# Reordering an attention and expert-layer kernel: one weight part loaded earlier, batch 0's second layer by parts over four token blocks, batch 2's scores two slots later and batch 3's attention three

## The chip, the cores and the metric

The kernel runs on one core of one Trainium2 chip. The metric is the device time of one execution in microseconds (us); lower is better. Each kernel was run several times and the medians are quoted. A ratio is the mean time of one kernel's fast runs over the mean of the other's fast runs of the same rounds, so it is not quite the ratio of the medians that stand beside it.

A core has a matrix engine (TensorE, "PE" in the profile, its weight loads "PEld"), VectorE ("DVE"), ScalarE ("ACT"), GpSimd ("POOL") and SyncE ("SP"). Each has its own list of instructions in the kernel; semaphores tie the lists together. In the trace TensorE holds to its list's order: in the changed kernel no matmul starts between 53.81 and 56.79 us, while the next of the list waits for `a`.

## The reference

For each of 8 batches and 8 heads there is a cross attention in both directions between 512 tokens `x` and 32 states. The results are stacked into 4352 rows of 512 numbers (8 batches of 512 tokens and 32 states) and go through a layer with 2048 hidden units:

```python
def _attn_ref(x, state):                      # x (8,8,512,64), state (8,8,32,64)
    scores = scale * x @ state^T;  a  = softmax(scores);  xread = a  @ state
    scores2 = scale * state @ x^T; a2 = softmax(scores2); sread = a2 @ x
    return concatenate([xread, sread], axis=2)

def _moe_ref(x, w_in, w_out, s, b):           # x (4352,512), w_in (512,2048), w_out (2048,512)
    h = x @ w_in
    r = maximum(h, 0)
    return (s * (r * r) + b) @ w_out
```

(The matrix products are abridged here; the softmax subtracts the row's maximum.) Outputs and inputs are float32; the kernel works in float16 with float32 sums.

## The kernel before

The program of one batch, in the names that the profile shows:

- `xT`: tokens transposed; by TensorE for batches 0 and 1 (`xTps`), by a transposing DMA later.
- `T` (scores), `E = exp(T)` on ScalarE, `D` (row sums by a matmul with a block of ones), `L = Ln(D)`, `R = exp(-L)`, `a = E*R` on VectorE. This is one chain of five steps over three engines.
- `M` = states times w_in, in four column groups. So the first layer of the tokens is `h = M^T a`, sixteen pieces of two 512-column matmuls: `mm1_x(b, f)`. ScalarE makes `r = relu(h)`, VectorE `g = r*r`.
- Second layer: for batch 0 in sixteen "units" of four 512-column matmuls, one token block and one quarter of w_out each. From batch 1 on by seven half-size products (`oA`, `oB`, `oC`, 112 matmuls of 256 columns), which need sums of quarters of `g` (`s`) and of w_out (`wd`) from VectorE.
- `V`, `sr`, `srT`: the states' own attention; all batches' states go through the layer at the end (names with `_sr`).
- The matmuls of `M` and `T` carry 64*32 in the profile and those of `V` 128*32, where the layers' carry 128*128; the prediction calls the first two kinds quarter-array and the layers' full-array.

TensorE's list is set by hand. "Slot f of batch s" below is the place in its list after `mm1_x(s, f)`. Into the sixteen slots of a batch go the second layer of the batch before and the attention of the batch after:

```python
def pieces(s):                                   # what goes into the slots of batch s, beside the second layer
    nb = s + 1
    if s == 1:
        ...
        at(2, lambda: att_M(1, 2, "act"))
        at(3, bias_sum)
        at(4, bias_end)
        at(3, lambda: att_M(1, 3, "act"))
        at(6, lambda: att_stT(2))
        ...
        at(8, lambda: att_M(2, 0, "act"))
        at(8, lambda: att_M(2, 1, "act"))
        at(10, lambda: att_M(2, 2, "act"))
        at(10, lambda: att_T(2, [0, 1]))
        at(11, lambda: att_ET(2))
        at(12, lambda: att_D(2, [0, 1]))
        at(13, lambda: att_M(2, 3, "act"))
        at(13, lambda: att_V(0))
        return out
    ...
# batch 0's second layer: token block, quarter
    units.append((0, 2 * (i // 8) + i % 2, i % 8 // 2))     # two blocks at a time, all four quarters
# slots of batch 1: one unit in each but 5, 14 and 15; then sixteen matmuls of batch 1's own second layer
    for f in [*range(5), *range(6, 14)]:
        items[f] = [lambda u=todo.pop(0): unit(u)]
    items[14], items[15] = first[0:8], first[8:16]
# loads, one queue, in this order (the first three w_in parts stand ahead of them)
    load_x(1); load_wi(3); load_wo(0..3); states; load_x(2)
```

PSUM, where matmuls write, is used as three pools of two buffers of 128x1024 float32 or less: `psA` for attention, `psH` for `h`, `psO` for the second layer. A buffer is free again when VectorE or ScalarE has copied it out (in e1, below, `h` waits 1.1 us for that).

The softmax here doesn't subtract the row's maximum and nothing guards it: scores larger than these inputs give would overflow.

## Time and profile before

| | value | where it is read |
|---|---|---|
| time | 212.24 us before the prediction (3 runs), 212.37 us in the pair with the change (4 runs) | device times |
| TensorE busy | 202.6 of 209.8 us | page, part 1 |
| TensorE's share of the chain that ended last | 88% | page, part 4 |
| TensorE's waits over 0.15 us | 3.2 us, all before 22 us | table of waits |
| one 512-column matmul at full clock | 0.216 us start to start | timeline |

The page of the kernel before: busy time, share of the span and count of instructions by engine (part 1), and the shares of the chain that ended last by engine (part 4).

```profile
PE 202.6 (97%) x1972; PEld 131.5 (63%) x1972; DVE 155.9 (74%) x286; ACT 132.1 (63%) x226; POOL 37.6 (18%) x64
...
PE 88%; DVE 4%; DMA 3%; ACT 3%; POOL 0%; issue 0%; SPq 0%
```

The table of waits of the kernel before, the three longest of TensorE's six rows: who waited, for whom, us in total, times, longest.

```profile
PE warm_ps L68 <- DVE warm L617: 1.2, 1, 1.2
PE h L68 <- DVE M L263: 0.6, 1, 0.6
PE T L68 <- ACT xT L187: 0.4, 1, 0.4
...
```

All six waits fall into the first 22 us, where w_in still arrives. After that, and until the tail, TensorE never stands idle, which makes the case simple to reason about: waiting time can only be won in the first 22 us (and in the tail), and anything that makes TensorE wait later can be expected to add to the total.

The next view cuts the same execution into stages, from the first matmul of one batch's first layer to the next one's: 0, 1, 2, then 3 to 6 together, then the rest. The columns are the stretch, its length, and for each engine busy us and count, then the granted TensorE clock as a share of full speed, the DMA share and GB/s.

```profile
11.55:27.17 15.62, 14.01 (x119) 5.68 (x118) 11.95 (x22) 13.42 (x26) 3.00 (x4) 1.00 1.28 205
27.17:52.25 25.08, 25.01 (x220) 11.18 (x218) 17.76 (x32) 18.16 (x29) 4.47 (x7) 1.00 1.17 161
52.25:74.81 22.56, 22.56 (x266) 15.27 (x264) 19.03 (x37) 15.89 (x26) 3.49 (x5) 1.00 0.72 125
74.81:162.30 87.49, 87.49 (x918) 59.92 (x916) 68.31 (x121) 63.62 (x105) 12.58 (x18) 1.00 0.50 96
162.30:209.80 47.50, 43.71 (x395) 35.30 (x392) 34.21 (x66) 15.30 (x33) 5.39 (x8) 1.00 0.19 62
```

Stage by stage TensorE's busy time equals the length to within 0.1 us, except in batch 0's stage and in the tail. The 87.49 us are four stages of 21.87 us: the steady state.

Last, the timeline of the kernel before at the chain from D to `a` of batch 2 (start, length, instruction; the rest of that stretch is cut):

```profile
46.26 0.59 PE L68 MATMUL D<-E,bones 128*128 128x512 f16 x2
...
46.95 1.02 ACT L240 ACTIVATE L<-D 128x1024 f32<-128x1024 f32 x1
...
48.00 1.06 ACT L241 ACTIVATE R<-L 128x1024 f16<-128x1024 f32 x1
...
49.09 0.69 DVE L242 TENSOR_TENSOR a<-E,R 128x1024 f16<-128x1024 f16 x1 [0.59 <-ACT R L241]
```

From the start of `D` at 46.26 to the end of `a` at 49.78 are 3.5 us. TensorE has three more slots, 6 us, to work through before batch 2's first layer needs `a` at 52.25, so nobody waits.

### The profile page before, as it was taken

What the parts mean: (1) busy time and instruction counts of PE and PEld (TensorE: products, weight loads), DVE (VectorE), ACT (ScalarE), POOL (GpSimd) and SP (SyncE); (2) the same over time, 40 slices, a digit from 0 to 9 for tenths busy, and PEclk for the clock granted to TensorE, in tenths of its full rate; (3) what the DMA queues carried; (4) which work ended last, traced back from release to release, by engine and by line L of the source; (5) the groups of instructions that cost most, each with busy time, mean ns of one, the idle gap of its engine ahead of it and who ended that gap; (6) DMA issues with size and microseconds to landing.
All of it is one profiled execution on the core that took longest, in us unless ns stands there. A gap on an engine that the chain in (4) does not pass through costs nothing.

```text
span 209.8 us, 4787 instructions
## 1 busy us (share of the span) xinstructions
PE 202.6 (97%) x1972; PEld 131.5 (63%) x1972; DVE 155.9 (74%) x286; ACT 132.1 (63%) x226; POOL 37.6 (18%) x64
## 2 busy tenths in 40 slices
PE   7988999999999999999999999999999999999992
PEld 2434343445666776677666766676667777788882
DVE  0587826978779895779677976698669977895862
ACT  2678865798597549964896479656984454533100
POOL 5870001501011312021111201120111111100210
PEclk9999999999999999999999999999999999999999
DMA  5999996999788393971199209211411111110143
GB/s 177 226 202 206 206 191 106 169 192 161 195 78 125 105 148 66 170 152 67 36 138 181 85 22 181 71 50 53 100 53 50 53 50 50 53 50 0 53 139 113
DMA packets 39289, 23.73 MB, mean 113 GB/s; under 512 B 24228, under 2 KB 37284, under 8 KB 39268
## 3 DMA queue, kind: packets, MB, share of 16 engines
q0 software_dynamic: 15536, 16.19, 40.1%
q1 hardware_dynamic: 22932, 6.88, 19.9%
q10 hardware_dynamic: 800, 0.36, 0.7%
q8 instruction: 15, 0.25, 0.5%
q14 instruction: 6, 0.05, 0.1%
HBM read 17.33 MB, written 8.91 MB: 125 GB/s over the span
## 4 chain that ended last, share of the span: by engine, by line
PE 88%; DVE 4%; DMA 3%; ACT 3%; POOL 0%; issue 0%; SPq 0%
PE h L68 25%; PE oB L68 18%; PE oC L68 12%; PE oA L68 11%; PE o L68 6%; PE Mps L68 4%; PE h_sr L68 3%; DMA xf<-in_x_dram 3%; ACT r L324 2%; PE D L68 1%; PE T L68 1%; PE V L68 1%; PE oB_sr L68 1%; DVE g L330 1%; DVE M L263 1%; PE oA_sr L68 1%
## 5 line engine op out<-in xcount | busy, mean ns | idle before, releaser
L324 ACT ACTIVATE r<-h 128x512 f16<-128x512 f32 x126 | 73.8, 600 | 47.3 <-PE h L68 45.6
L68 PE MATMUL h<-a,M 128*128 128x512 f16 x256 | 75.0, 379 | 0.9 <-DVE M L263 0.6
L330 DVE TENSOR_TENSOR g<-r 128x1024 f16<-128x1024 f16 x64 | 43.9, 688 | 16.0 <-ACT r L324 15.9
L68 PEld LDWEIGHTS <-s 128*128 128x128 f16 x448 | 42.8, 98 | 17.6 <-issue 3.7
L68 PEld LDWEIGHTS <-g 128*128 128x128 f16 x400 | 37.9, 98 | 18.2 <-issue 2.9
L495 POOL DMA_DIRECT2D out_dram<-osb x27 | 18.2, 675 | 127.2 <-DVE osb L487 119.8
L68 PE MATMUL oB<-wd,s 128*128 128x256 f16 x224 | 32.7, 273 | 0.0
L68 PE MATMUL oA<-wo,g 128*128 128x256 f16 x224 | 31.6, 273 | 0.1
L68 PEld LDWEIGHTS <-M 128*128 128x128 f16 x256 | 24.6, 98 | 10.8 <-DVE M L263 1.6
L266 ACT CAST M<-Mps 128x1024 f16<-128x1024 f32 x27 | 26.8, 1019 | 1.4 <-PE Mps L68 0.8
L68 PE MATMUL oC<-wd,s 128*128 128x256 f16 x112 | 16.5, 273 | 0.0
L68 PE MATMUL o<-wo,g 128*128 128x512 f16 x64 | 16.3, 380 | 0.0
L68 PE MATMUL oB<-wd,g 128*128 128x256 f16 x112 | 15.9, 273 | 0.0
L68 PE MATMUL oC<-wo,s 128*128 128x256 f16 x112 | 15.3, 273 | 0.0
L68 PE MATMUL Mps<-wi,stT 64*32 64x512 f16 x256 | 12.2, 383 | 0.0
L324 ACT ACTIVATE r_sr<-h_sr 128x256 f16<-128x256 f32 x16 | 6.1, 382 | 8.4 <-PE h_sr L68 8.4
L68 PEld LDWEIGHTS <-stT 64*32 64x32 f16 x384 | 4.6, 89 | 10.4 <-issue 8.1
L487 DVE SCALAR_TENSOR_TENSOR osb<-oC,s_bc,u 128x512 f32<-128x512 f32 x12 | 9.0, 749 | 2.7 <-PE oC L68 2.7
L430 DVE TENSOR_TENSOR s<-s,g 128x1024 f16<-128x1024 f16 x14 | 9.6, 687 | 0.2
L217 ACT ACTIVATE E<-T 128x512 f16<-128x512 f32 x16 | 9.4, 596 | 0.5 <-PE T L68 0.5
L432 DVE TENSOR_TENSOR s<-g,s 128x1024 f16<-128x1024 f16 x14 | 9.6, 686 | 0.0
L68 PE MATMUL h_sr<-srdT,wi 128*128 128x256 f16 x64 | 9.6, 273 | 0.0
(96 smaller groups left out, 201.1 us busy)
## 6 DMA issues: line engine op xcount, KB each, us to landing
out_dram<-osb POOLq DMA_DIRECT2D x31, 256.0 KB, 2.5
xn<-in_x_dram POOLq DMA_DIRECT2D x7, 512.0 KB, 9.5
wi<-in_moe_w_in_dram POOLq DMA_DIRECT2D x4, 512.0 KB, 9.1
wo<-in_moe_w_out_dram POOLq DMA_DIRECT2D x4, 512.0 KB, 15.9
xf<-in_x_dram SPq DMA_DIRECT2D x2, 512.0 KB, 4.9
out_dram<-osb_sr SPq DMA_DIRECT2D x8, 32.0 KB, 1.6
out_dram<-osb_sr ACTq DMA_DIRECT2D x8, 32.0 KB, 1.7
out_dram<-osb_last SPq DMA_DIRECT2D x2, 128.0 KB
```

The lines of the kernel that those rows point to most:

```text
L68: return nc.tensor.matmul(out, lhsT, rhs, start=start, stop=stop, tile_position=tp, is_transpose=is_transpose, skip_group_check=True,)
L217: nc.scalar.activation(a["E"][:, g, :].rearrange("p (m t) -> p m t", m=2), T[:, :, 256 * i : 256 * i + 256], AF.Exp, scale=scale, accum_ou ...
L263: nc.vector.tensor_copy(dst[:, 0], two[0])
L266: nc.scalar.copy(dst, ps)
L324: nc.scalar.activation(r16[:, f % 2], hps, AF.Relu)
L330: nc.vector.tensor_mul(gt[:, f % 4 - 1 : f % 4 + 1], r16, r16)
L430: nc.vector.tensor_sub(o, SQ[b, 1, j], a11)
L432: nc.vector.tensor_sub(o, a12, SQ[b, 2, j])
L487: nc.vector.scalar_tensor_tensor(osb, acc[bank], s_bc, add, ALU.mult, ALU.add)
L495: nc.gpsimd.dma_start(dst[j][:, :, n0 : n0 + NH], osb)
```

## The change

The intent: with the first w_out quarter loaded early, batch 0's second layer can start while batch 0's first layer still waits for copies, filling TensorE's early idle time. All four token blocks are then worked quarter by quarter, so that each quarter of w_out is used as it lands. Blocks 2 and 3 take one attention PSUM buffer for that long, so attention must make room: batch 2's scores move two slots down in batch 1's slots, part of its other work moves into batch 2's own slots, and there batch 3's attention moves three slots down. The diff, cut to its core:

```diff
@@ loads
         cast_st(nc.gpsimd, 1, 2)
+        load_wo(0)
         load_x(1)
         load_wi(3)
-        for q in range(4):
+        for q in range(1, 4):
             load_wo(q)
+        load_x(2)
         nc.gpsimd.dma_start(out=st16[:, 4:, 0, :], in_=st_v[:, 4:, :])
-        load_x(2)
@@ units: four token blocks, quarter by quarter; blocks 2 and 3 in an attention buffer
-        units.append((0, 2 * (i // 8) + i % 2, i % 8 // 2))
+        units.append((0, i % 4, i // 4))
...
-        if f0 == 0:
+        if f0 == 0 and rr < 2:
             ops_of[key, rr] = psO.tile([P, DM], FP32, tag="o", name=f"o_{key}_{rr}")
+        elif f0 == 0 and rr == 2:
+            both = att_ps([P, 2, DM], FP32, f"o_{key}_2")
+            ops_of[key, 2], ops_of[key, 3] = both[:, 0], both[:, 1]
@@ slots of batch 0
-            9: [lambda: att_xT_pe(1, 0), lambda: att_xT_pe(1, 1)],
-            10: [lambda: att_T(1, [0, 1])],
+            8: [unit0(0)],
+            10: [lambda: att_xT_pe(1, 0), lambda: att_xT_pe(1, 1)],
             11: [
-                lambda: att_M(0, 3, "split"),
-                lambda: att_M(1, 0, "dve"),
+                lambda: att_T(1, [0, 1]),
+                lambda: att_M(0, 3, "dve"),
+                unit0(1),
                 lambda: att_D(1, [0, 1]),
             ],
-            13: [ ... units 0 and 1 ],
-            15: [lambda: att_M(1, 1, "act"), ... unit 2],
+            13: [lambda: att_M(1, 0, "dve"), unit0(2), unit0(3)],
+            15: [unit0(4), unit0(5)],
@@ slots of batch 1
-                at(8, lambda: att_M(2, 0, "act"))
-                at(8, lambda: att_M(2, 1, "act"))
-                at(10, lambda: att_M(2, 2, "act"))
-                at(10, lambda: att_T(2, [0, 1]))
-                at(11, lambda: att_ET(2))
-                at(12, lambda: att_D(2, [0, 1]))
-                at(13, lambda: att_M(2, 3, "act"))
-                at(13, lambda: att_V(0))
+                at(8, lambda: att_stT(2))
+                at(8, lambda: att_M(1, 3, "act"))
+                at(10, lambda: att_M(2, 0, "act"))
+                at(10, lambda: att_M(2, 1, "dve"))
+                at(12, lambda: att_T(2, [0, 1]))
+                at(13, lambda: att_ET(2))
+                at(14, lambda: att_D(2, [0, 1]))
...
-                for f in [*range(5), *range(6, 14)]:
-                    items[f] = [lambda u=todo.pop(0): unit(u)]
-                items[14], items[15] = first[0:8], first[8:16]
+                for f in range(9):
+                    us = [todo.pop(0) for _ in range(1 + (f == 0))]
+                    items[f] = [lambda u=u: unit(u) for u in us]
+                for f in range(9, 16):
+                    items[f] = first[2 * (f - 9) : 2 * (f - 9) + 2] if f < 15 else first[12:16]
@@ slots of batch 2 (d = 3 there, 0 later): batch 3's attention d slots down, and
+            if s == 2:
+                at(1, lambda: att_M(2, 2, "act"))
+                at(1, lambda: att_M(2, 3, "act"))
+                at(3, lambda: att_V(0))
+                at(3, lambda: att_V(1))
...
-                if (s == 1 and 5 <= f < 12) or (s == 2 and f == 6):            # VectorE's w_out differences
+                if (s == 1 and f in (9, 11, 13, 15)) or (s == 2 and f in (1, 2, 6, 7)):
@@ tail
-                    eng = nc.sync if i % 2 else nc.scalar
+                    eng = nc.gpsimd if i % 2 else nc.scalar
```

Left out: which engine copies `xT` and one half of an `M` group, which PSUM pool batch 1's `xTps` and `D` use, when the finished blocks are copied out, and the slots of batch 1's own `M` groups and the bias (they move by one to five slots) and of two token sums (from batch 1's slots 7 and 9 to batch 2's 2 and 3).

More of the change, by code (lines that the diff above doesn't have):

```diff
@@ L171, in att_xT_pe @@
         else:
-            pool, tag = (psA, "att") if g else (psO, "o")
-            two = [pool.tile([P, 512], FP16, tag=tag, name=f"xTps_{b}_{g}_{i}") for i in range(2)]
+            ps = att_ps([P, 1024], FP16, f"xTps_{b}_{g}")
+            two = [ps[:, 512 * i : 512 * i + 512] for i in range(2)]
         for q in range(NQ):
@@ L185, in att_xT_pe @@
         for i in range(2):
-            eng = nc.scalar.copy if i == 1 and (b, g) != (0, 1) else nc.vector.tensor_copy
+            act = i == 1 and g == 0 if b == 0 else g == 1
+            eng = nc.scalar.copy if act else nc.vector.tensor_copy
             eng(
@@ L228, in att_D @@
         g0 = gs[0]
-        if b == 0:
+        if b < 1:
             Dps = psH.tile([P, n, S], FP32, tag="h", name=f"D_{b}_{g0}")
@@ L263, in att_M @@
             nc.vector.tensor_copy(dst[:, 0], two[0])
-            (nc.vector.tensor_copy if c in (0, 3) else nc.scalar.copy)(dst[:, 1], two[1])
+            (nc.vector.tensor_copy if c == 0 else nc.scalar.copy)(dst[:, 1], two[1])
         elif how == "act":
@@ L399, in mm2_part @@
             late.append(lambda: evac(ops, key, rr, 0, DM, dmas_of(key, rr, nc.gpsimd)))
-            if bias_ready:
-                late.pop()()
+            if bias_ready and rr != 2:
+                while late:
+                    late.pop(0)()
     def weight_sums():
@@ L679, with unit0 @@
         mm1_x4(0, 0, lambda: att_M(0, 1, "split"))
+        def unit0(i):
+            return lambda: unit(units[i])
         b0 = {
             5: [lambda: att_M(0, 2, "split")],
-            9: [lambda: att_xT_pe(1, 0), lambda: att_xT_pe(1, 1)],
-            10: [lambda: att_T(1, [0, 1])],
+            8: [unit0(0)],
+            10: [lambda: att_xT_pe(1, 0), lambda: att_xT_pe(1, 1)],
             11: [
-                lambda: att_M(0, 3, "split"),
-                lambda: att_M(1, 0, "dve"),
+                lambda: att_T(1, [0, 1]),
+                lambda: att_M(0, 3, "dve"),
+                unit0(1),
                 lambda: att_D(1, [0, 1]),
             ],
-            13: [
-                lambda: unit(units[0]),
-                lambda: unit(units[1]),
-            ],
-            15: [lambda: att_M(1, 1, "act"), lambda: unit(units[2])],
+            13: [lambda: att_M(1, 0, "dve"), unit0(2), unit0(3)],
+            15: [unit0(4), unit0(5)],
         }
@@ L699 @@
                 fn()
-        todo = units[3:]
+        todo = units[6:]
         def gated_x3():
@@ L720, in pieces @@
                 at(12, lambda: load_x(4))
-                at(2, lambda: att_M(1, 2, "act"))
-                at(3, bias_sum)
-                at(4, bias_end)
-                at(3, lambda: att_M(1, 3, "act"))
-                at(6, lambda: att_stT(2))
-                at(10, bias_half)
-                at(8, lambda: att_M(2, 0, "act"))
-                at(8, lambda: att_M(2, 1, "act"))
-                at(10, lambda: att_M(2, 2, "act"))
-                at(10, lambda: att_T(2, [0, 1]))
-                at(11, lambda: att_ET(2))
@@ L732, in pieces @@
-                at(12, lambda: att_D(2, [0, 1]))
-                at(13, lambda: att_M(2, 3, "act"))
-                at(13, lambda: att_V(0))
+                at(1, lambda: att_M(1, 1, "act"))
+                at(3, lambda: att_M(1, 2, "act"))
+                at(5, bias_sum)
+                at(6, bias_end)
+                at(8, lambda: att_stT(2))
+                at(8, lambda: att_M(1, 3, "act"))
+                at(10, lambda: att_M(2, 0, "act"))
+                at(10, lambda: att_M(2, 1, "dve"))
@@ L735, in pieces @@
+                at(12, lambda: att_T(2, [0, 1]))
+                at(13, lambda: att_ET(2))
+                at(14, lambda: att_D(2, [0, 1]))
+                at(14, bias_half)
                 return out
+            d = 3 if s == 2 else 0
             if s + 3 < B:
                 at(13 if s == 2 else 9, lambda: load_x(s + 3))
+            if s == 2:
[3 more added lines that the diff above has]
+                at(3, lambda: att_V(1))
@@ L738, in pieces @@
             if nb < B:
-                at(0, lambda: att_stT(nb))
-                at(3, lambda: att_T(nb, [0, 1]))
-                at(3, lambda: att_M(nb, 0, "act"))
-                at(4, lambda: att_ET(nb))
+                at(d + (s == 2), lambda: att_stT(nb))
+                at(d + 3, lambda: att_T(nb, [0, 1]))
+                at(d + 3, lambda: att_M(nb, 0, "act"))
+                at(d + 4, lambda: att_ET(nb))
                 if nb + 1 < B:
-                    at(4, lambda: att_xT_dma(nb + 1))
@@ L745, in pieces @@
-                at(5, lambda: att_D(nb, [0, 1]))
-                at(7, lambda: att_M(nb, 1, "act"))
-                at(7, lambda: att_M(nb, 2, "act"))
+                    at(d + 4, lambda: att_xT_dma(nb + 1))
+                at(d + 5, lambda: att_D(nb, [0, 1]))
+                at(d + 7, lambda: att_M(nb, 1, "act"))
+                at(d + 7, lambda: att_M(nb, 2, "act"))
             if s == 2:
-                at(1, lambda: att_srT(0))
-                at(8, lambda: att_V(1))
-                at(12, lambda: att_srT(1))
@@ L752, in pieces @@
-            at(10, lambda: att_V(s))
-            at(11, lambda: att_srT(s))
+                at(5, lambda: att_srT(0))
+                at(5, lambda: att_srT(1))
+            at(d + 10, lambda: att_V(s))
+            at(d + 11, lambda: att_srT(s))
             if nb < B:
-                at(10, lambda: att_M(nb, 3, "act"))
+                at(d + 10, lambda: att_M(nb, 3, "act"))
             if s == last_b:
@@ L779 @@
                 mm1_x(s, f)
+                if s == 2 and f in (2, 3):
+                    with tc.issue_after(G["last"]):
+                        token_sum(1, 3, f - 2)
                 if s == 2 and f in (8, 9):
@@ L785 @@
                 if s in fast:
-                    if f in ((7, 9) if s == 1 else (7, 11)):
+                    if f in ((7, 11) if s > 1 else ()):
                         with tc.issue_after(G["last"]):
```

## The prediction

> **What bounds it now.** TensorE is busy 97% of the span (page, part 1) and makes 88% of the chain of waits. The table of waits holds six waits of TensorE, 3.2 us in all, none after 22 us; from there matmuls start back to back (timeline: a 512-column one every 0.216 us). What start times show as lost later are mostly switches between full-array and quarter-array matmuls: about 0.22 us for a lone attention group (at 25.64 us).[...] The change keeps TensorE's work, so only 1.5 to 2.5 us of early waits can be won, and each new wait is added time.
>
> **What the change moves, costed.**
>
> 1. Loads. The queue is full until 34 us: a 1 MB part lands every 2.4 to 3.2 us. The first w_out part takes the place of batch 1's x, so x1 lands near 19.8 us (was 17.3) and the fourth w_in part near 22.9 us (was 20.5). Batch 1's transposes (were at 17.9) wait for x1, its scores for two ScalarE copies (0.6 us each), batch 0's last weights for w_in. One early quarter unit (0.86 us) fills part. Walking the order, batch 1's first layer starts at 30.35 us; before it was 27.17, plus 2.15 us of work moved ahead (three units less one attention group): 29.3. Lost: about 1.0 us.
>
> 2. Token blocks 2 and 3 hold one of two attention PSUM buffers through batch 1's stage. There batch 2's state transpose, copied by VectorE, must leave the other before the next group: 0.5 us. D of batch 2 waits about 0.25 us for E.
>
> 3. The largest: D of batch 2 moves to slot 14, two slots before batch 2's first layer, and these slots are short (two or four 0.11 us matmuls beside 0.43 us). From D's start to the end of a (D, Ln, exp, product) the trace takes 3.5 us (46.26 to 49.78); in the new ScalarE order a relu stands between Ln and exp: 4.1 us. TensorE has 1.5 us of work there and is in order[...]. New wait: about 2.6 us.
>
> 4. VectorE work (weight differences, token sums, V) moves into batch 2's first slots: qa, u and the V evictions come late: about 1 us of waits in slots 4 and 5.
>
> 5. Split attention groups: about +0.4 us of switches. The tail's DMAs from GpSimd instead of SyncE: under 0.1 us.
>
> **Sum.** 1.0 + 0.75 + 2.6 + 1.0 + 0.4 = 5.75 us, all on TensorE's line. A little off for overlap: **217.4 us, range 214.5 to 219.8; faster 0.01, within 2% 0.27, slower 0.72.**
>
> **What would show it.** Waits of TensorE or its weight loads: batch 1's xTps on x1 until about 19.8 us; T on ScalarE; Mps on w_in near 22.9 us; h on VectorE's a, 2 to 3 us, near 53 to 56 us; stTps and oB on VectorE near 62 to 64 us. From batch 3 on each stage takes as before (22 us).
>
> **What would make it wrong.** If the first w_out part and x1 land earlier than their places say; if the a-chain of batch 2 overlaps more than the order shows; if early units fill more of the early waits than I see. Then it is within 2%.

1.0 + 0.75 + 2.6 + 1.0 + 0.4 = 5.75 us, and with 0.6 us off for overlap 212.24 us become 217.4. The 0.22 us for a lone group can be followed in the trace of the kernel before: from the start of the last matmul ahead of it (25.64 us) to the first behind it (26.30) are 0.66 us; one 512-column matmul takes 0.22 of them, and the group, if its eight 64*32 matmuls are counted by area as one of 128*128 (an estimate), another 0.22. That the rest is lost at a switch is the author's reading of it; what happens there the trace doesn't show. The 0.4 us of item 5 is an estimate, about two such groups.

## The result, and the profile after

The changed kernel took 221.34 us (220.79 to 222.01, 4 runs) against 212.37 us (211.69 to 212.69, 4 runs): a ratio of 1.043, with a 95% interval of 1.038 to 1.047. It is slower, as predicted, but by 9.0 us where 5.2 were forecast, and outside the range of 214.5 to 219.8.

The page of the changed kernel: the same two lines, and between them the granted TensorE clock in tenths over 40 slices of 5.5 us.

```profile
PE 205.9 (94%) x1972; PEld 131.9 (60%) x1972; DVE 157.1 (71%) x286; ACT 131.4 (60%) x225; POOL 41.8 (19%) x72
...
PEclk9999999999699999999999999999999999999997
...
PE 72%; DVE 8%; DMA 8%; ACT 6%; issue 2%; POOL 1%; SPq 0%
```

TensorE still does all its 1972 matmuls, but its share of the chain that ended last fell from 88% to 72%. Two things stand out: its busy time *rose* by 3.3 us although its work is the same, and one slice of the clock reads 6 instead of 9. (The 7 at the end is the tail; no matmul starts in the last 2.5 us.)

The table of waits of the changed kernel, TensorE's rows (those that the kernel before has too are cut, and one of 0.3 us before batch 0's first layer):

```profile
PE h L68 <- DVE a L243: 2.7, 1, 2.7
...
PE srT L68 <- DVE sr L294: 1.2, 1, 1.2
PE xTps L68 <- DMA xn<-in_x_dram: 1.0, 1, 1.0
...
PE stTps L68 <- DVE sr L294: 0.5, 1, 0.5
PE Mps L68 <- DVE stT L156: 0.4, 1, 0.4
...
PE bias_ps L68 <- DVE wsum L584: 0.4, 1, 0.4
PE oB L68 <- DVE u L521: 0.3, 1, 0.3
...
```

The stages of the changed kernel, cut as before:

```profile
11.71:30.77 19.06, 16.96 (x124) 6.78 (x123) 12.15 (x21) 13.16 (x25) 2.66 (x4) 1.00 1.29 204
30.77:56.79 26.02, 22.49 (x168) 9.75 (x167) 15.53 (x26) 15.96 (x26) 5.23 (x8) 1.00 1.14 163
56.79:84.24 27.45, 25.50 (x311) 15.95 (x311) 22.16 (x43) 17.70 (x28) 3.61 (x5) 0.94 0.42 82
84.24:171.73 87.49, 87.49 (x918) 59.91 (x916) 68.24 (x120) 63.62 (x105) 11.90 (x17) 1.00 0.47 92
171.73:220.03 48.30, 43.71 (x395) 35.29 (x392) 34.21 (x66) 15.28 (x33) 9.36 (x16) 0.97 0.19 61
```

Batches 3 to 6 take 87.49 us in both kernels, to the hundredth. The clock of 0.94 in batch 2's stage is the dip; the 0.97 of the last row comes from the last 2.5 us of the span, recorded at half clock. All the loss lies before them and in the tail:

| stretch | before | after | work moved (estimate) | lost |
|---|---|---|---|---|
| up to batch 0's first layer | 11.55 | 11.71 | 0 | 0.2 |
| batch 0's first layer to batch 1's | 15.62 | 19.06 | +2.15 in | 1.3 |
| batch 1's to batch 2's | 25.08 | 26.02 | 2.15 and 1.0 out | 4.1 |
| batch 2's to batch 3's | 22.56 | 27.45 | +1.0 in | 3.9 |
| batches 3 to 6 | 87.49 | 87.49 | 0 | 0.0 |
| rest | 47.50 | 48.30 | 0 | 0.8 |

The moved work is worked out from the timeline before: 2.15 us are three units of 0.865 us less one attention group; 1.0 us are two `M` groups and a `V`, with their switches. The sum, 10.2 us before rounding, is the difference of the two profiled executions (220.0 less 209.8 us), which is 1.2 us more than that of the medians: most unprofiled runs of the kernel before have a span near 210.6 us rather than 209.8, and the profiled one of the changed kernel was among its two slower ones.

Where the 4.1 us of batch 1 went, the timeline of the changed kernel shows, at the same chain as before:

```profile
52.33 0.61 PE L68 MATMUL D<-E,bones 128*128 128x512 f16 x2
...
53.34 1.05 ACT L241 ACTIVATE L<-D 128x1024 f32<-128x1024 f32 x1
...
54.25 0.64 ACT L325 ACTIVATE r<-h 128x512 f16<-128x512 f32 x1
54.73 1.11 ACT L242 ACTIVATE R<-L 128x1024 f16<-128x1024 f32 x1
...
56.05 0.69 DVE L243 TENSOR_TENSOR a<-E,R 128x1024 f16<-128x1024 f16 x1
...
56.79 0.76 PE L68 MATMUL h<-a,M 128*128 128x512 f16 x2 [2.71 <-DVE a L243]
```

The chain is 4.4 us long here, from 52.33 to 56.74, because ScalarE had two relus before `L` and one between `L` and `R` (about 0.3 us later each), and VectorE was at its last `g` when `R` was done (0.2). TensorE had three short groups to do beside it (2, 2 and 4 matmuls) and then stood idle until 56.79. That is the wait of 2.71 us, predicted as 2.6. Of the other 1.4 us of the 4.1, 0.74 are the waits of `Mps` on `stT` and of `bias_ps`; the rest, 0.6 us, is TensorE busy for longer than the moved work explains.

Of the 3.9 us of batch 2, half (1.95 us) are the waits of `srT`, `stTps` and `oB`; most of the rest went another way. These are two stretches of 3.41 us of the changed kernel, the second of them the one in which the profile records a halved clock (columns as in the stages):

```profile
53.68:57.09 3.41, 0.70 (x6) 0.39 (x5) 3.41 (x7) 2.15 (x3) 0.00 (x0) 1.00 1.56 142
57.09:60.50 3.41, 3.41 (x27) 1.37 (x25) 2.11 (x4) 1.17 (x2) 0.00 (x0) 0.50 0.22 43
```

In the first, TensorE is busy for 0.70 us and otherwise idle (the wait for `a`). In the second it is busy all the time, at clock 0.50. 3.41 us at half speed are 1.7 us lost. The prediction had nothing of this. It is also half of why "busy" rose by 3.3 us: slow matmuls count as busy. (The other 1.6 us are busy time beyond the moved work: 0.8 in batch 0's stage, 0.6 in batch 1's, 0.2 in batch 2's. No run takes it apart; the added switches of the split attention groups would be in it.) In this stretch a 256-column matmul takes 0.21 us start to start instead of 0.11.

### The profile page after: what moved, and what is told of

It reads as the page before. It is cut to its first block, busy times and chain, and to the rows that moved or that the text cites. A ratio compares the mean times of both kernels' runs of the same rounds, so it can differ in the third digit from the quotient of the medians.

```text
span 220.0 us, 4787 instructions
## 1 busy us (share of the span) xinstructions
PE 205.9 (94%) x1972; PEld 131.9 (60%) x1972; DVE 157.1 (71%) x286; ACT 131.4 (60%) x225; POOL 41.8 (19%) x72
## 4 chain that ended last, share of the span: by engine, by line
PE 72%; DVE 8%; DMA 8%; ACT 6%; issue 2%; POOL 1%; SPq 0%
PE h L68 20%; PE oB L68 16%; PE oC L68 10%; PE oA L68 10%; DMA xn<-in_x_dram 5%; PE o L68 5%; PE Mps L68 3%; ACT r L325 3%; PE h_sr L68 3%; DMA xf<-in_x_dram 2%; DVE g L331 2%; ACT E L218 1%; PE oB_sr L68 1%; DVE osb L373 1%; PE D L68 1%
## 5 line engine op out<-in xcount | busy, mean ns | idle before, releaser
L68 PE MATMUL oB<-wd,s 128*128 128x256 f16 x224 | 33.5, 278 | 0.3 <-DVE u L521 0.3
L68 PE MATMUL oA<-wo,g 128*128 128x256 f16 x224 | 32.5, 273 | 0.1
L267 ACT CAST M<-Mps 128x1024 f16<-128x1024 f32 x26 | 25.8, 1018 | 1.0 <-PE Mps L68 0.3
L68 PE MATMUL Mps<-wi,stT 64*32 64x512 f16 x256 | 12.7, 394 | 0.5 <-DVE stT L156 0.4
L429 DVE TENSOR_TENSOR s<-g 128x1024 f16<-128x1024 f16 x14 | 9.6, 685 | 0.0
```

The lines of the kernel that those rows point to most:

```text
L68: return nc.tensor.matmul(out, lhsT, rhs, start=start, stop=stop, tile_position=tp, is_transpose=is_transpose, skip_group_check=True,)
L267: nc.scalar.copy(dst, ps)
L429: nc.vector.tensor_sub(o, a11, a21)
```

## The experiments

Twelve kernels were run, all correct. Each is an edit of the kernel before or of the changed kernel ("after"). "Ratio" is against the kernel before, run on the same chip in the same rounds (212.1 to 212.4 us in every group).

| run | base | what it does | median us | ratio (95%) |
|---|---|---|---|---|
| after | | the change | 221.34 | 1.043 (1.038 to 1.047) |
| e1 | after | batch 2's D three slots earlier | 219.90 | 1.036 (1.034 to 1.038) |
| e2 | after | the wait filled with idle matmuls | 219.84 | 1.035 (1.034 to 1.037) |
| e3 | after | tail back on SyncE | 221.95 | 1.045 (1.039 to 1.051) |
| e4 | after | w_out differences earlier | 222.55 | 1.049 (1.047 to 1.052) |
| e5 | before | new loads alone | 213.88 | 1.009 (1.005 to 1.012) |
| e6 | before | tail on GpSimd alone | 212.45 | 1.001 (0.999 to 1.003) |
| e7 | before | attention shift alone | 214.56 | 1.012 (1.009 to 1.015) |
| e8 | after | batch 2's V earlier | 221.43 | 1.043 (1.041 to 1.046) |
| e9 | before | e5, e6 and e7 together | 217.73 | 1.026 (1.023 to 1.028) |
| e10 | after | units spread over batch 1's slots | 220.66 | 1.039 (1.037 to 1.041) |
| e11 | before | two lone attention groups joined | 215.33 | 1.014 (1.010 to 1.017) |
| e12 | before | one of them joined | 211.81 | 1.000 (0.998 to 1.002) |

### Does the idle stretch halve the clock? (e2)

```diff
             for f in range(NKF):
+                if s == 2 and f == 0:
+                    warm_up(12)          # twelve 512-column matmuls that nobody reads
                 mm1_x(s, f)
```

> The changed kernel with twelve idle 512-column matmuls (2.6 us of TensorE work whose result nobody reads) just before batch 2's first layer, so that the wait for a stays but TensorE is not idle in it. Theory (the idle stretch is what lowers the clock): h of batch 2 still starts near 56.8 us, the granted clock stays 1.0 through 57 to 61 us, and the kernel gains 1.5 to 1.9 us: about 219.6 us. Rival (the low clock has another cause than the idle stretch): the low stretch of 3.4 us stays and the time stays at 221 us.

The same two stretches of this kernel:

```profile
53.68:57.09 3.41, 3.29 (x17) 1.54 (x16) 3.41 (x7) 1.83 (x4) 0.00 (x0) 1.00 1.44 126
57.09:60.50 3.41, 3.41 (x39) 2.07 (x38) 3.37 (x6) 2.81 (x5) 0.00 (x0) 1.00 0.18 39
```

TensorE is no less blocked, since the first-layer matmul still starts at 56.36 us, yet the clock stays 1.00 and batch 2's stage takes 25.92 us instead of 27.45. The kernel gained 1.5 us, 219.84 against 221.34. The theory holds here: with 0.70 us busy in the first stretch the clock of the second was 0.50, with 3.29 us busy it was 1.00, and the price of the wait was 2.7 us plus 1.5 to 1.7 us. Matmuls that do nothing useful bought the second part back. The other kept traces with the same waits in that stage, or nearly so (e8), sort the same way: batch 2's stage takes 27.45 to 27.65 us in the three profiled executions with a low window in it (the changed kernel, e3, e8), and 25.84 to 25.92 us in e2, e4 and e10, which have none. (Whole runs do not sort so neatly: e8's run at a mean clock of 0.996 was its slowest, 221.88 us.)

### Is the wait on `a` a matter of the slot of D? (e1)

```diff
-                at(10, lambda: att_M(2, 0, "act"))
-                at(10, lambda: att_M(2, 1, "dve"))
-                at(12, lambda: att_T(2, [0, 1]))
-                at(13, lambda: att_ET(2))
-                at(14, lambda: att_D(2, [0, 1]))
+                at(9, lambda: att_T(2, [0, 1]))
+                at(10, lambda: att_ET(2))
+                at(11, lambda: att_D(2, [0, 1]))
+                at(12, lambda: att_M(2, 0, "act"))
+                at(14, lambda: att_M(2, 1, "dve"))
```

> The changed kernel, but batch 2's T, E transpose and D stand at slots 9, 10 and 11 of batch 1 (were 12, 13, 14) and its first two weight groups at 12 and 14 (were both 10). Theory (the chain from D to a is 4.1 us long and TensorE had 1.5 us of work beside it; the idle stretch then costs a slow-clock stretch of 3.4 us at half speed): the 2.7 us wait of h on a goes or falls under 0.7 us, the granted clock has no low stretch near 57 to 60 us, and the kernel gains 3.5 to 4.5 us: about 217 to 218 us where the change gave 221.3. Rival (a is late because VectorE is behind with sums): most of the wait stays, gain under 1 us.

The wait on `a` is gone and the clock has no low stretch. But the kernel gained 1.4 us instead of 3.5 to 4.5: no more than the clock. The table of waits of e1 has two rows that the changed kernel doesn't have in this size:

```profile
PE oB L68 <- DVE s L435: 1.4, 1, 1.4
PE h L68 <- ACT r L325: 1.4, 2, 1.1
```

The `h` row is two waits for a PSUM buffer that ScalarE's relu frees, 1.1 us of it at slot 15 of batch 1; the `oB` row is batch 2's first slot, waiting for a token sum of VectorE. So the wait on `a` hid two others that end at about the same time. Behind it ScalarE and VectorE had not finished the work of batch 1's last slots either. This expectation missed: the step that failed was to take one wait as the whole hold-up.

### Is VectorE's backlog the cause? (e4)

```diff
-                if (s == 1 and f in (9, 11, 13, 15)) or (s == 2 and f in (1, 2, 6, 7)):
+                if s == 1 and f < 8:
```

> The changed kernel with all eight weight differences of VectorE in slots 0 to 7 of batch 1, where VectorE was busy 2 of 10 us, instead of four in slots 9 to 15 and four in batch 2. Theory (the waits of TensorE on VectorE in batch 2, for stTps, oB and srT, 2.0 us in all, come from VectorE's backlog, but the wait of h on a comes from the chain through ScalarE): the waits for stTps, oB and srT fall under 0.5 us together, the wait on a stays over 2.4 us, the low clock stays, and 1 to 2 us are gained: about 219.5 us. Rival (VectorE's backlog makes a late): the wait on a shrinks by 1 us or more.

TensorE's waits in e4:

```profile
PE h L68 <- DVE a L243: 2.8, 1, 2.8
...
PE srT L68 <- DVE sr L294: 1.2, 1, 1.2
PE Mps L68 <- DVE osb L373: 1.0, 1, 1.0
PE Mps L68 <- DVE stT L156: 1.0, 1, 1.0
...
PE bias_ps L68 <- DVE wsum L584: 0.8, 1, 0.8
...
```

Both halves are told apart. The wait on `a` stays (2.8 us), so VectorE's sums don't make it. But the waits that were to go stayed as well: `srT` 1.2, and `stTps` and `oB` at 0.5 and 0.3 us as before. New ones came in batch 1's first slots, where the differences stood in front of the bias and of PSUM copies: `bias_ps` 0.8, two `Mps` 1.0 us each. The kernel got slower, 222.55 us. VectorE had idle time there (busy 5.3 of 14.2 us in slots 0 to 7 of the changed kernel; the expectation's 2 of 10 us holds for the first ten), but the differences stood in its list in front of copies that TensorE waits for, and those waits grew by 0.4 to 1.0 us. This miss says that the waits in batch 2 have nothing to do with where the w_out differences stand.

The profiled run of e4 held a second lesson. Its wait was as long as in the changed kernel, and yet its clock stayed at 1.00:

```profile
54.81:58.22 3.41, 1.56 (x10) 0.87 (x9) 3.07 (x6) 3.31 (x5) 0.00 (x0) 1.00 1.53 166
58.22:61.63 3.41, 2.50 (x29) 1.32 (x29) 2.20 (x5) 1.27 (x3) 0.00 (x0) 1.00 0.20 40
```

The clock records change on a grid of 3.41 us: the changed kernel's stretches at full clock last 51.20 and 157.01 us, 15 and 46 times 3.413, its low one 3.413, and that of the kernel before 204.80, 60 times. In e4 the grid happened to cut the idle stretch in two: 1.56 of 3.41 us busy in one window, 2.50 in the next, with the clock at 1.00 in both. In the changed kernel one window held nearly all of it (0.70 busy). So the same wait came with a low clock in one execution and not in the other, by its place on the grid; e4's own four runs differ as well (below). Of the whole windows in the span of the changed kernel two are followed by half clock, this one and one in the tail (214.10 to 217.51 us, 1.40 us busy); in all others, from 5.89 us on, TensorE was busy for 2.24 us or more, and in all those of the kernel before for 2.54 us or more. (Busy time is as the profile models it. These are the cases seen; at what busy time the change comes was not tested.) e11, below, has a low window in mid-run too, with a wait of 2.6 us:

```profile
48.04:51.45 3.41, 1.37 (x44) 0.52 (x42) 2.76 (x5) 2.95 (x4) 0.55 (x1) 1.00 1.42 150
51.45:54.86 3.41, 2.86 (x38) 1.34 (x38) 1.95 (x7) 0.00 (x0) 0.00 (x0) 0.50 1.08 270
```

This raises a rival for e2: its profiled execution lies elsewhere on the grid, and its wait alone, unfilled, might have left the clock full too. The run-by-run clocks speak against luck. In the four runs of e4 the mean clock was 0.996, 0.996, 0.989 and 0.992; in the four of the changed kernel it was 0.987 to 0.992 in all, and in e2 never below 0.996. (One low window is 0.8% of a run, and the kept traces without one before the tail read 0.996 or more; so 0.992 or less is read as one: four of four runs of the changed kernel, three of four of e3 and of e8, two of four of e4, none of e2's four.)

### Parts of the change alone, on the kernel before (e5, e6, e7)

e5 has the diff's first hunk and nothing else.

> The kernel before with nothing but the new order of loads (first w_out part fourth, x2 ahead of the states). Theory (x1's place in the queue sets when batch 1's transposes start, and TensorE is in order): the transposes wait on x1 for about 2.5 us (17.9 to about 20.5 us), batch 1's first layer starts 2 to 3 us later than 27.2, all later stages keep their length, the time rises by 2 to 3 us to about 215 us, and the clock stays full. Rival (the order of loads is free, since the states and w_out are needed later): under 0.5 us.

TensorE's waits in e5, the row that the kernel before lacks:

```profile
PE xTps L68 <- DMA xn<-in_x_dram: 2.5, 1, 2.5
```

x of batch 1 landed at 20.38 us (17.29 before), and TensorE, in order, stood at its transposes until then. Batch 1's first layer started at 29.55 us instead of 27.17; every later stage kept its length. In time it cost 0.85% (1.6 us between the medians, 2.4 us between the profiled executions), somewhat less than the 2 to 3 us expected. The landing times of this and two other profiled runs, in us from the span's start:

```
                 w_in 3rd   4th in queue     5th             6th
before            14.65     x1     17.29     w_in 4th 20.47  w_out 1st 22.85
after             14.35     w_out  16.82     x1       20.49  w_in 4th  22.93
e5 (loads alone)  14.27     w_out  16.81     x1       20.38  w_in 4th  22.91
```

e6 has the diff's last hunk and nothing else.

> The kernel before with nothing but the second half of the state rows' output DMAs on GpSimd. Theory (GpSimd's closing drain runs about 4 us past its last DMA issue): from the last matmul's start to the end 4.8 us instead of 4.0, the time rises by 0.6 to 1.0 us to about 213.2 us. Rival (the tail of the changed kernel is longer for another reason): no change.

In the profile the time from the last matmul's start to the end was 4.49 us (4.00 before, 4.80 in the changed kernel), so 0.5 us, not 0.8. In time there is nothing to see: 1.001, between 0.999 and 1.003. The interval ends at about 0.6 us, so of the expected 0.6 to 1.0 us only the lowest end is left.

e7 moves batch 2's and 3's attention as the change does, with the rest as before:

```diff
-                at(10, lambda: att_M(2, 2, "act"))
-                at(10, lambda: att_T(2, [0, 1]))
-                at(11, lambda: att_ET(2))
-                at(12, lambda: att_D(2, [0, 1]))
-                at(13, lambda: att_M(2, 3, "act"))
-                at(13, lambda: att_V(0))
+                at(12, lambda: att_T(2, [0, 1]))
+                at(13, lambda: att_ET(2))
+                at(14, lambda: att_D(2, [0, 1]))
...                                    # and batch 2's slots as in the change, d = 3
```

> The kernel before with nothing but the attention of batch 2 (T, E, D at slots 12, 13, 14 of batch 1, its last two weight groups and both V at slots 1 and 3 of batch 2, batch 3's attention three slots down); the second layer of batch 0, the loads and the tail are as before, so the last slots of batch 1 keep their eight 0.11 us or four 0.216 us matmuls. Theory: the chain from D to a (3.5 us, no relu between here) has 2.6 us of TensorE work beside it, so h waits 0.7 to 1.2 us on a[...], so the clock stays full; the waits of batch 2 for stTps, oB and srT on VectorE (0.5, 0.3, 1.2 us) come with the shift and appear here too: 2 to 3.5 us in all, about 214.5 to 216 us. Rival (those waits come from the short last slots of batch 1 and the sums moved out of it): only the wait on a, about 213.3 us.

Two rows of TensorE's waits in e7:

```profile
PE srT L68 <- DVE sr L293: 1.2, 1, 1.2
PE h L68 <- DVE a L242: 0.8, 1, 0.8
```

These are what the shift costs by itself: 0.8 us on `a` (2.7 in the whole change), and the whole 1.2 us of `srT`. Batch 2's stage took 25.24 us, 1.0 us of it moved work. 2.2 us were lost in time, 1.2%. So the wait of `srT` comes with the shift and not with the short slots; it stands 14 slots into batch 2 and wasn't in the prediction. The rival, that only the wait on `a` would appear, falls. Of the other two expected waits `oB` appears (0.3 us) and `stTps` does not.

### What is behind the wait of srT? (e8)

```diff
-            at(d + 10, lambda: att_V(s))
-            at(d + 11, lambda: att_srT(s))
+            at(9 if s == 2 else 10, lambda: att_V(s))
+            at(12 if s == 2 else 11, lambda: att_srT(s))
```

> The changed kernel with batch 2's own V at slot 9 and its transpose at slot 12 of batch 2 (were 13 and 14). Theory (at slot 13 the two V copies of VectorE stand behind the token sums of slots 11 to 13 and the transpose one slot later waits for them): the 1.2 us wait of srT on VectorE goes, batch 2's stage shortens by 0.6 to 1.2 us, low clock and the wait on a stay. Rival (VectorE is simply full in batch 2): another wait of the same size appears in its place.

A row of TensorE's waits in e8:

```profile
PE Mps L68 <- DVE sr L294: 1.3, 1, 1.3
```

The rival is right here. `srT` waits no more, but an `M` group now waits 1.3 us for the same two `sr` copies, whose PSUM buffer it needs. The time is unchanged (221.43). VectorE is nearly full around `sr` in batch 2 once everything is three slots down (busy 11.36 of 11.65 us in slots 8 to 14 of the changed kernel); moving one consumer moves the wait.

### Do the parts add up, and what is the rest? (e9, e10)

e9 is the kernel before with e5, e6 and e7 together. It lacks the second layer by parts.

> The kernel before with the three parts tried alone put together: the new order of loads, the shifted attention of batch 2, and the tail on GpSimd; batch 0's second layer as before. Against the changed kernel it lacks only the four token blocks by parts (and the slots and copies that go with them). Theory (the parts add up, and the rest, 4 to 5 us, belongs to the second layer by parts with its short last slots): 0.85 + 1.2 + 0.1% over the kernel before, so about 217 us; the wait of h on a 0.8 us, no low clock, the wait of srT 1.2 us. Rival (the loads and the attention shift hurt each other): 219 us or more.

217.73 us, 1.026; the three alone sum to 1.021 (0.85, 1.2 and 0.1%). So about half a per cent more than a plain sum: nearly additive. (In the profiled executions the three alone add 5.5 us to the kernel before and e9 adds 5.7.) Its waits are those of e5 and e7 (`xTps` 2.6, `srT` 1.2, `a` 0.8), and its profiled run has no low clock. The other 3.6 us, up to 221.34, belong to the second layer by parts, with the slots, copies and sums that were moved with it; this is found by subtraction, no run has that part alone. Read from the two profiles, they are: the wait on `a` 2.7 instead of 0.8 us (1.9), the low clock (1.7), `Mps` on `stT` 0.4, `bias_ps` 0.4, `stTps` on `sr` 0.5, less 1.3 us that the early units do win. The first stage took 18.25 us in e9 and 19.06 less 2.15 us of moved work in the change. That sums to 3.6 us; but the two profiled executions differ by 4.5 us. About 0.5 us more of TensorE busy time in batch 1's stage, and 0.5 us before batch 0's first layer and in the tail, are not in the list, so that it meets the difference of the medians is in part chance.

So the change's own idea works as far as it goes: units in batch 0's slots fill 1.3 us of the wait that the new loads open. But the ten units that were left then went into slots 0 to 8 of batch 1, and slots 9 to 15 were left with 0.65 us of TensorE's work each. e10 spreads them:

```diff
-                for f in range(9):
-                    us = [todo.pop(0) for _ in range(1 + (f == 0))]
-                    items[f] = [lambda u=u: unit(u) for u in us]
-                for f in range(9, 16):
-                    items[f] = first[2 * (f - 9) : 2 * (f - 9) + 2] if f < 15 else first[12:16]
+                for f in (0, 1, 2, 3, 4, 6, 8, 10, 12, 13):
+                    items[f] = [lambda u=todo.pop(0): unit(u)]
+                items[14], items[15] = first[0:8], first[8:16]
...
-                at(10, lambda: att_M(2, 0, "act"))
+                at(9, lambda: att_M(2, 0, "act"))
```

> The changed kernel with batch 0's last ten units spread over slots 0, 1, 2, 3, 4, 6, 8, 10, 12, 13 of batch 1 and the first sixteen 0.11 us matmuls of batch 1's second layer in slots 14 and 15, where the change has the units in slots 0 to 8 and the sixteen in slots 9 to 15; batch 2's first two weight groups at slots 9 and 10. Theory (slots 9 to 15 are too short for ScalarE's and VectorE's work of that stretch, and for the chain from D to a): the wait on a falls from 2.7 to 1.2 to 1.8 us, the clock stays full, waits on PSUM buffers in slots 9 to 12 may cost up to 1 us; 2 to 3 us gained, about 218.5 us. Rival (the shape of the slots doesn't matter, ScalarE and VectorE are full anyway): under 0.7 us beyond what the clock gives.

Four of TensorE's waits in e10, three of them known from the changed kernel:

```profile
PE h L68 <- DVE a L243: 1.2, 1, 1.2
PE bias_ps L68 <- DVE wsum L584: 1.2, 1, 1.2
...
PE Mps L68 <- DVE stT L156: 1.1, 1, 1.1
PE Mps L68 <- ACT M L267: 0.7, 1, 0.7
```

The wait on `a` fell to 1.2 us and the clock stayed full, as expected. Yet only 0.7 us were gained: slots 5, 7, 9 and 11 now had no unit, and the waits at slots 6, 8 and 10 grew (`bias_ps` 0.4 to 1.2, `Mps` on `stT` 0.4 to 1.1, a new one on ScalarE's copy of `M`, 0.7). The mechanism was right and the net gain was missed. With one attention buffer held by blocks 2 and 3, TensorE's filler can be moved about but is missing somewhere. What e10 can't show is how much of these waits the held buffer makes and how much the missing filler, since both are in it.

### The tail (e3)

```diff
-                    eng = nc.gpsimd if i % 2 else nc.scalar
+                    eng = nc.sync if i % 2 else nc.scalar
```

> The changed kernel with the second half of the state rows' output DMAs back on SyncE instead of GpSimd. Theory (GpSimd's last drain runs 4 us past its last DMA issue and ends last): from the last matmul's start to the end of the span 4.0 us instead of 4.8, GpSimd's drain no longer last, 0.7 to 0.8 us gained. Rival (the tail differs by where the outputs land): 4.8 us stays.

In the profile the tail took 3.78 us from the last matmul's start (4.80 in the changed kernel). In time it shows nothing: 221.95 us with a range of 220.34 to 223.62, a wider spread than any other run's, which is not explained (one of its runs took 222.37 at a full clock). Over all profiled executions the tail took 4.25 to 4.80 us in the eight kernels with GpSimd (mean 4.5) and 3.78 to 4.00 us in the six with SyncE (mean 3.9). So the profile gives it about 0.5 us, and neither e3 nor e6 shows a timed difference.

GpSimd's closing drain is recorded from about its last output DMA's issue on: in the changed kernel for 4.1 us, from 215.17 to 219.25 us, 0.7 us past SyncE's; in the kernel before for 3.7 us, from 200.32 to 203.98, long before the end. That it sets the end is read from the order of the records and not tested further.

### A version that beats both? (e11, e12)

By the prediction's reading both kernels pay for switches between full-array and quarter-array matmuls, about 0.22 us for the lone group at 25.64 us of the kernel before. e11 joins two lone attention groups of the kernel before to others:

```diff
-            15: [lambda: att_M(1, 1, "act"), lambda: unit(units[2])],
+            15: [lambda: att_M(1, 1, "act"), lambda: att_M(1, 2, "act"), lambda: unit(units[2])],
...
-                at(2, lambda: att_M(1, 2, "act"))
...
-                at(13, lambda: att_V(0))
+                at(13, att_V01)              # batch 0's and 1's V in one PSUM tile
...
-                at(8, lambda: att_V(1))
```

> The kernel before with two lone quarter-array groups joined to others: batch 1's third weight group beside its second at slot 15 of batch 0, and batch 1's V beside batch 0's in one PSUM tile. Theory (each lone group costs about 0.2 us of switches, TensorE has no slack): 0.3 to 0.5 us in the profile, 0.2%, so 212.0 us, within noise. Rival (the switches are hidden): nothing, or a loss where copies come late.

TensorE's longest wait in e11:

```profile
PE V L68 <- DVE sr L299: 2.6, 1, 2.6
```

It lost 2.9 us. The first pair did save something in the profile: from slot 14 of batch 0 to slot 5 of batch 1 it took 10.91 us against 11.19 over the same work. But the second V's matmuls waited 2.6 us for VectorE to read the first V out of the tile they share, and in the worse of the six runs the clock fell as well (mean clock 0.989 to 1.0; the run at 1.0 has a span of 212.4 us, those at 0.992 or below 214.0 to 214.9). e12 keeps the first half only:

> The kernel before with only the first half of e11: batch 1's third weight group beside its second at slot 15 of batch 0. In e11's profile this stretch (first-layer slot 14 of batch 0 to slot 5 of batch 1) took 10.91 us where the kernel before took 11.19. Theory (one pair of tiling switches saved, nothing waits on it): 0.2 to 0.3 us shorter in that stretch, every later stage as before, about 212.1 us against 212.4: 0.1%, which five rounds may not tell from nothing. Rival (a later wait takes it back): the stretch is shorter but batch 2's first layer starts as late as before.

211.81 us, ratio 1.000 (0.998 to 1.002): the same time. In the profile batch 1's stage took 24.59 us instead of 25.08, of which 0.2 us had moved ahead, but batch 2's took 22.88 instead of 22.56, where its scores now waited 0.2 us for a transposing DMA. So no version was found that beats the kernel before by a measurable amount.

## Why the prediction was wrong

The direction and the main mechanism held; the sum was too small. It forecast 5.2 us and 9.0 came. Point by point:

1. **"Lost: about 1.0 us" by the loads.** In the ledger 1.3 us (plus 0.2 before it). x1 landed at 20.49 us where 19.8 was expected, so TensorE's wait for it was longer; w_in's last part came at 22.93, as forecast (22.9). Of the signs named for this stretch, the scores waited on VectorE's copy of `xT` (0.46 us, a weight load) and not on ScalarE's, and `Mps` shows no wait over 0.15 us, though it began 0.05 us after w_in landed. Alone (e5) the loads cost 1.6 us in time.
2. **"0.5 us" for the state transpose and "0.25 us" for D.** The first came as 0.38 us of wait, 0.55 start to start. D of batch 2 waited less than the table lists; instead the bias matmul waited 0.36 us on VectorE, which was not foreseen.
3. **"New wait: about 2.6 us" on `a`.** It was 2.71 us. The chain was 4.4 us long, not 4.1, and TensorE's work from D on 1.75 us (4.46 from D's start to the first layer's, less 2.71), not 1.5.
4. **"About 1 us of waits in slots 4 and 5".** 0.47 and 0.31 us, where and on what was said. But the step stopped at slot 5. At slot 14 `srT` waited 1.17 us for the same engine, and e7 shows that this comes with the shift of the attention.
5. **"The tail's DMAs ... under 0.1 us".** In the profile it was 0.5 us on average (0.8 in this execution), in time too little to show. The "0.4 us of switches" can't be read off singly: beyond waits, moved work and low clock the ledger leaves 0.9 us of TensorE busy time in batches 1 and 2.

The step that failed is the **"Sum. 1.0 + 0.75 + 2.6 + 1.0 + 0.4"**: it counted each wait at its own length and let TensorE go on at full speed after it. The clock records show that it did not. The idle stretch of item 3 was followed by 3.41 us at half clock, 1.7 us, and e2 shows that the idle stretch was the cause: filled with useless matmuls, the same wait left the clock alone and the kernel was 1.5 us faster. Beside it stand terms left out (`srT` 1.2, the bias 0.4, the tail 0.5) and the 0.6 us taken off "for overlap" (5.75 less the 5.16 between 212.24 and 217.4). Together that is about 4.4 us where the forecast was 3.8 short: two of its own terms came out smaller, and the terms are read from two executions 10.2 us apart, not 9.0. The clock is the largest term and not the whole: with the clock full (e2) the kernel still takes 219.84 us, 2.4 above the forecast and just past the end of its range. "From batch 3 on each stage takes as before" held exactly: 87.49 us.

What is known of the clock here is what the records show. In the changed kernel it was 0.50 for 3.413 us after a window with 0.70 of 3.41 us busy; TensorE was busy throughout the low window, and the next one was at full clock. The prediction doesn't mention the clock, and the kernel before could not have shown it: its clock was full over its whole span, and in no whole window of its 3.41 us grid was TensorE busy for less than 2.54 us.

Also in the prediction and found true: TensorE kept to its list's order, so each wait blocked all that stood behind it (no matmul between 53.81 and 56.79 us).

## What to carry to other kernels

When the busiest engine has no slack, price a reordering by its chains: for each result that moves later, compare the chain's length in the trace with the work that is left for that engine beside it. Then look for what comes after the wait: another engine that is just as late (e1), a buffer still held (e8, e10), and a granted clock that falls after the wait (0.50 for 3.41 us here, e2). If a wait like the one of 2.7 us here can't be avoided, filling it with matmuls that nobody reads is worth trying, as it gave back 1.5 us here.
